# Attention, Fourier mixing and two FFNs on one core: token transform over two tiles at once, exp's bias of two batches on GpSimd, second W1 by column halves, a new priority table

## The chip, the cores and the metric

The kernel runs on one core of a Trainium2 chip. The metric is the device time of one execution, in microseconds; the time of a kernel is the median of several runs. Engines are named as the profile names them: PE (TensorE), DVE (VectorE), ACT (ScalarE), POOL (GpSimd) and SP (SyncE, which issues all DMAs here).

## What is computed

Three stages follow each other, for 4 batches of 576 tokens:

```
scores = (q @ k.T) / 8                    # 8 heads of 64
keep the 32 largest of each row, the rest to -1e9
x = softmax(scores) @ v                   # heads side by side: [576, 512]
u = x + real(fft(fft(x, axis=1), axis=2))
x = u + relu(norm(u) @ w_ch1) @ w_ch2     # 512 -> 2048 -> 512
x = x + relu((norm(x) * g) @ w_ch1b) @ w_ch2b
```

The weights come in as 64-bit floats and are split on the chip into a high and a low half-precision part; products use three of the four combinations.

## The kernel before

**Tiles.** A batch's tokens lie in two pairs of 128-row tiles, `xA` and `xB` (each 128 x 2 x 512), and a rest of 64 rows in `xC`, which two batches share. Row pairs that the transform adds and subtracts lie in the same partition of `xA` and `xB`.

**Attention.** `attend` works on 128 rows of one head (a *round* here; 36 rounds a batch, 144 in all). PE makes the scores (`ps`), ACT copies them (`s`), DVE finds the 32 largest by four MAX8 (`mx`) and three MATCH_REPLACE8 (`w`). A one-column DVE instruction makes `nb`, the bias of exp (lines 850 and 851). ACT does Prelu (needs the 32nd largest only), then Exp (needs `nb`), then the half-precision copy `p`; POOL subtracts for the low part, SP transposes by DMA into `pt`, PE multiplies with `vt` into `xp`, ACT scales into the tiles. There are four buffers of `s`, and two each of `w`, `p` and `pt`. Before a batch's first round its scales (`sc`) must be known: `stats` loads q, k, v in 27 pieces, PE sums squares, `find_scales` ends on DVE. `prep` then scales and transposes q and k.

**Token transform.** `fourier_rows(b, half)` folds the rows (line 944): for the cosine and the sine part, and for each of the two 128-row tiles and the rest, one instruction adds or subtracts `xA` and `xB` (`z`), one folds `z` on itself (`f`), ACT copies one column, ACT writes the high part, DVE the low part (`unT`). Then PE multiplies with a constant matrix. `fourier_columns` finishes, `do_norm` prepares the first FFN.

**FFN.** `ffn` goes over 16 blocks of 128 hidden units, `f` = 0 to 15: 12 matmuls of the first weight, relu on ACT (`h`, and `hr` for the low part), then 6 matmuls of the second weight into `acc`, for tile pairs A and B and, every second batch, C.

**Weights.** Four weights, 1a, 2a (first FFN), 1b, 2b (second FFN). Each is fetched in 16 pieces, turned to 32-bit on ACT, DVE and POOL, its scale is found, and eight chunks are converted. For 1b ACT makes a scaled copy in `ws` (two buffers), then its high part, and POOL the low part. 1b is converted into the place (`W1B`) that serves 2b as staging before, so its pieces come after 2b.

**The order.** Nothing runs in the order in which the code is written. Every call is recorded, and `Program.order` (line 336) places all instructions with a planner: at each step the engine and the instruction that can start first by the planner's own costs (`price`, line 289), ties by a priority from `LEVELS` (ten numbers for each of 51 stages: five levels, five slopes) and earliest times from `PACE` and `P.at`. The result is a fixed list for each engine, which the engine works through in order. In the trace all these instructions therefore have one line, 433.

Of the kernel before, what the change touches and what calls it, by code (L numbers as in the profile page):

```python
# [63 lines left out]
SMALL = "dve"  # L64
FLIP = "gp"
# [131 lines left out]
class Program:  # L197
# [91 lines left out]
    def price(self, op, out, reads, size, es):  # L289
# [11 lines left out]
        elif e == "vector":  # L301
            fast = op.method in ("tensor_scalar", "tensor_copy") and not psum
            fields = sum(isinstance(op.kw.get(k), View) for k in ("scalar", "scalar1", "scalar2"))
            op.cost = (168 if op.method == "match_replace" else 76 if op.method in ("tensor_scalar", "tensor_tensor") else 66) + 57 * fields + n / (1.92 if fast else 0.96)
        elif e == "scalar":
            fields = sum(isinstance(op.kw.get(k), View) for k in ("scale", "bias", "accum_out"))
            op.cost = (68 if psum else 110) + 0.834 * n + 94 * fields
        elif e == "gpsimd":
            half = any(v.at(0).dtype in (F16, BF16) for v in reads + [out])
            if op.method in ("tensor_tensor", "scalar_tensor_tensor"):  # L310
                op.cost = 650 if n < 4 else 168 + 1.886 * n if half else 160 + 2.12 * n
            elif op.method in ("tensor_scalar", "tensor_copy"):
# [23 lines left out]
    def order(self):  # L336
# [29 lines left out]
        while todo:  # L366
# [27 lines left out]
            if op.eng == "tensor":  # L394
                k = int(t // window)
                if columns.get(k - 1, 0) < enough:
                    op.cost *= 2
                k = int((t + op.cost) // window)
                columns[k] = columns.get(k, 0) + op.columns
# [36 lines left out]
class _Engine:  # L436
    def __init__(self, prog, name):
        self._p, self._n = prog, name

    def __getattr__(self, method):  # L440
        return lambda *a, **k: self._p.record(self._n, method, a, k)


@with_exitstack
def tile_attention_fourier_ffn(ctx: ExitStack, tc: tile.TileContext, q, k, v, w1a, w2a, g, w1b, w2b, c1_in, c2_in, c2l_in, out):
    nc = tc.nc
    outf = out.rearrange("b s d -> (b s) d")
    P = Program(tc, ctx)
    pe, dve, act, gp, sp = P.pe, P.dve, P.act, P.gp, P.sp
    sm, rv = getattr(P, SMALL), getattr(P, FLIP)  # L450
# [787 lines left out]
```

## Time and profile before

| | us |
|---|---|
| median of 3 runs (1319.77 to 1326.45) | 1324.66 |
| the profiled execution | 1330.46 |
| its span, first to last instruction | 1328.7 |
| busy: PE / DVE / ACT / POOL | 1182.6 / 993.0 / 846.0 / 680.2 |
| mean granted clock of PE | 0.940 |

The profile has one execution. Its rows give busy time by stretch (windows), by instruction shape (groups), in order of time (timeline), and the chain of work that ended last. PEclk is the granted clock as a share of 2.4 GHz. A busy PE is not PE at its peak: matmuls overlap, so a row's mean duration is longer than the step from one matmul to the next.

### The profile page before, as it was taken

The page shows a single profiled execution, that of the slowest core. Times are in us where ns is not written, and L with a number is a line of the kernel's source. Part 1 is how long each engine was busy: PE and PEld are TensorE (multiplying, and loading weights), DVE is VectorE, ACT ScalarE, POOL GpSimd, SP SyncE. Part 2 cuts the span into 40 slices and gives each one's busy share as a digit, 9 for nine tenths or more (in the row PEclk, how much of TensorE's full clock was granted, in tenths as well). Part 3 has the DMA queues.
Part 4 walks back from the last instruction along what each step waited for, and adds up shares of the span by engine and source line. Part 5 has one row for each costly group of instructions (what it writes and reads, how often), then busy time and mean ns, then how long its engine had stood idle before and what let it go on. Part 6 is the DMA issues. An engine that isn't in the chain of part 4 may idle for free.

```text
span 1328.7 us, 27154 instructions
## 1 busy us (share of the span) xinstructions
PE 1182.6 (89%) x9422; PEld 748.8 (56%) x9422; DVE 993.0 (75%) x2361; ACT 846.0 (64%) x1888; POOL 680.2 (51%) x1015
## 2 busy tenths in 40 slices
PE   7757888676799749999999999979999999999998
PEld 3433444342566525656666766656666666667665
DVE  6999999939899998999967986999996651214112
ACT  4658888467878897787767786777777652122111
POOL 3666343646777776666756564766645452011000
PEclk9999788578799869999999999999999999999999
DMA  6898655978867656876826376699514735014112
GB/s 186 193 263 222 178 129 122 264 189 234 196 162 158 121 120 153 174 170 141 177 62 110 68 175 164 141 217 189 105 22 97 163 90 129 13 24 126 27 33 56
DMA packets 356085, 184.86 MB, mean 139 GB/s; under 512 B 293225, under 2 KB 321002, under 8 KB 355818
## 3 DMA queue, kind: packets, MB, share of 16 engines
q1 hardware_dynamic: 355946, 183.11, 59.0%
q8 instruction: 74, 1.21, 0.4%
q14 instruction: 65, 0.53, 0.1%
HBM read 101.78 MB, written 14.16 MB: 87 GB/s over the span
## 4 chain that ended last, share of the span: by engine, by line
PE 63%; DVE 11%; DMA 7%; ACT 6%; issue 2%; POOL 2%; SPq 2%; POOLq 0%; ACTq 0%; DVEq 0%
PE mm L433 31%; PE acc L433 24%; PE ps L433 4%; PE xp L433 4%; DVE mx L433 4%; DVE w L433 3%; DMA pt<-p 2%; DMA ws<-W2D 2%; ACT s L433 2%; SPq L433 2%; DMA W1B<-in_moe_w_ch_dram 2%; DVE tiny L433 1%; DVE W1B L433 1%; DVE W2A L433 1%; ACT W1B L433 1%
## 5 line engine op out<-in xcount | busy, mean ns | idle before, releaser
L433 DVE MAX8 mx<-w 128x8 f32<-128x576 f32 x432 | 314.3, 747 | 1.3
L433 POOL TENSOR_TENSOR p<-s,p 128x64 f16<-128x64 f32 (+1 forms) x288 | 208.1, 743 | 118.2 <-ACT p L433 106.5
L433 ACT ACTIVATE h<-mm 128x256 f16<-128x256 f32 (+1 forms) x320 | 115.7, 362 | 212.7 <-PE mm L433 181.0
L433 PEld LDWEIGHTS <-h 128*128 128x128 f16 x1728 | 161.7, 98 | 141.6 <-issue 7.0
L433 PE MATMUL mm<-unT,W1B 128*128 128x256 f16 (+1 forms) x1920 | 220.7, 263 | 6.0 <-ACT W1B L433 3.4
L433 PE MATMUL mm<-unT,W1A 128*128 128x256 f16 (+1 forms) x1920 | 221.3, 263 | 1.1 <-DMA unT<-t2k 0.6
L433 PE MATMUL acc<-W2A,h 128*128 128x512 f16 x864 | 216.9, 379 | 1.4 <-POOL h L433 1.2
L433 POOL TENSOR_TENSOR h<-hr,h 128x256 f16<-128x256 f32 (+1 forms) x224 | 143.9, 646 | 140.1 <-ACT h L433 78.9
L433 PEld LDWEIGHTS <-W1B 128*128 128x128 f16 (+1 forms) x1984 | 176.8, 99 | 67.3 <-POOL W1B L433 13.9
L433 DVE MATCH_REPLACE8 w<-mx,w 128x576 f32<-128x576 f32 x288 | 212.8, 740 | 0.0
L433 PEld LDWEIGHTS <-W1A 128*128 128x128 f16 (+1 forms) x1984 | 177.5, 99 | 60.1 <-POOL W1A L433 8.1
L433 PE MATMUL acc<-ws,h 128*128 128x512 f16 x654 | 165.9, 380 | 6.2 <-DMA ws<-W2D 5.6
L433 DVE SCALAR_TENSOR_TENSOR h<-mm,h 128x256 f16<-128x256 f32 (+1 forms) x96 | 36.4, 379 | 171.8 <-ACT h L433 142.9
L433 DVE MAX8 mx<-s 128x8 f32<-128x576 f32 x144 | 107.5, 747 | 53.9 <-ACT s L433 53.6
L433 ACT ACTIVATE s<-s,mx 128x576 f32<-128x576 f32 x144 | 111.0, 773 | 22.2 <-DVE mx L433 21.9
L433 ACT ACTIVATE hr<-mm 128x256 f32<-128x256 f32 (+1 forms) x224 | 82.1, 368 | 65.0 <-PE mm L433 53.8
L433 PE MATMUL xp<-vt,pt 128*128 128x65 f16 (+1 forms) x2240 | 106.0, 203 | 16.5 <-DMA pt<-p 13.7
L433 PEld LDWEIGHTS <-pt 128*128 128x128 f16 (+1 forms) x2240 | 94.6, 107 | 44.9 <-DMA pt<-p 22.9
L433 ACT ACTIVATE s<-ps 128x576 f32<-128x576 f32 x144 | 93.6, 650 | 39.9 <-POOL p L433 21.8
L433 DVE MATCH_REPLACE8 w<-mx,s 128x576 f32<-128x576 f32 x144 | 106.6, 740 | 0.0
L433 PE MATMUL ps<-kt,qt 128*128 128x512 f16 (+5 forms) x512 | 90.2, 320 | 18.3 <-ACT s L433 18.2
L433 ACT ACTIVATE p<-s 128x576 f16<-128x576 f32 x144 | 97.6, 683 | 2.4 <-DMA pt<-p 1.9
(155 smaller groups left out, 1643.2 us busy)
## 6 DMA issues: line engine op xcount, KB each, us to landing
ws<-W2D SPq DMA_DIRECT2D x118, 256.0 KB
W1B<-in_moe_w_ch_dram SPq DMA_DIRECT2D x56, 512.0 KB
n<-in_q_dram SPq DMA_DIRECT2D x32, 128.0 KB
n<-in_k_dram SPq DMA_DIRECT2D x32, 128.0 KB
n<-in_v_dram SPq DMA_DIRECT2D x32, 128.0 KB
W2F<-W1B SPq DMA_DIRECT2D x16, 256.0 KB
ws<-in_moe_w_ch_dram SPq DMA_DIRECT2D x16, 256.0 KB
W1B<-W2F SPq DMA_DIRECT2D x16, 256.0 KB
```

The lines of the kernel that those rows point to most:

```text
L433: getattr(getattr(self.nc, op.eng), op.method)(*[fix(a) for a in op.args], **{k: fix(v) for k, v in op.kw.items()})
```

## The change

Five things change.

1. `fourier_rows` does both 128-row tiles with one instruction each: `z`, `f`, the column copy, the high and the low part. The 64-row rest keeps its own.
2. `nb` of batches 0 and 1 is made on POOL instead of DVE: 72 instructions of one column move.
3. 1b's eight chunks are converted in the order 0, 2, 4, 6, 1, 3, 5, 7: first those that hold the first half of the hidden units.
4. The planner's costs: a MATCH_REPLACE8 is 56 ns cheaper, and a matmul that it takes to be at the low clock costs twice its time plus 25 ns. The constants' earliest time goes from 183 to 210.
5. `LEVELS` and `PACE` have other numbers throughout.

```
-SMALL = "dve"
+SMALL = (0, 1)
...
-PACE = {'1a': (7.0, 4.0, 60.0, 6.5), '2a': (8.0, 5.0, 88.0, 1.5), '2b': (31.0, 10.0, 0.0, 8.5), '1b': (87.0, 14.0, 119.0, 9.5), 's1': (83.0, 4.5, 230, 0.5), 's2': (127.0, 3.0, 670, 8.0), 's3': (3.0, 1.0, 100, 2.5)}
+PACE = {'1a': (0.0, 3.5, 23.0, 1.0), '2a': (3.0, 6.5, 150.0, 8.5), '2b': (4.0, 3.5, 0.0, 2.0), '1b': (30.0, 13.0, 253.0, 0.0), 's1': (54.0, 7.0, 230, 0.5), 's2': (227.0, 5.0, 670, 8.0), 's3': (47.0, 0.0, 100, 2.5)}
...
-            op.cost = (168 if op.method == "match_replace" else 76 if op.method in ("tensor_scalar", "tensor_tensor") else 66) + 57 * fields + n / (1.92 if fast else 0.96)
+            op.cost = (112 if op.method == "match_replace" else 76 if op.method in ("tensor_scalar", "tensor_tensor") else 66) + 57 * fields + n / (1.92 if fast else 0.96)
...
-                    op.cost *= 2
+                    op.cost = 2 * op.cost + 25
...
-        for c in range(8):
-            P.at(t1 + c * step1, (nm, 2, c))
+        for i, c in enumerate(range(8) if nm != "1b" else (0, 2, 4, 6, 1, 3, 5, 7)):
+            P.at(t1 + i * step1, (nm, 2, i))
...
-            parts = [tmps(2 * c + j) for j in range(2)]
+            parts = [tmps(2 * i + j) for j in range(2)]
...
-        sm.tensor_scalar(out=nb, in0=mx[:, 31:32], scalar1=mx[:, 0:1], scalar2=scale(b, "c"), op0=ALU.subtract, op1=ALU.mult)
+        (gp if b in SMALL else dve).tensor_scalar(out=nb, in0=mx[:, 31:32], scalar1=mx[:, 0:1], scalar2=scale(b, "c"), op0=ALU.subtract, op1=ALU.mult)
...
+            z = P.tile("t2k", [128, 2, 257], F32)
+            f = P.tile("t2k", [128, 2, 129], F32)
+            if half:
+                eng.tensor_tensor(out=z, in0=x["A"][:, :, 128:385], in1=x["B"][:, :, 128:385], op=op, claim=xf)
+                eng.tensor_tensor(out=f[:, :, 0:128], in0=z[:, :, 0:128], in1=z[:, 0, 256:257].dims((257, 2), (-1, 128)), op=op)
+                act.activation(out=f[:, :, 128], in_=z[:, :, 128], func=AF.Copy)
...
+            act.activation(out=xf[:, cs, 0:2, 0, 0:n], in_=f[:, :, 0:n], func=AF.Copy, scale=sv)
+            dve.scalar_tensor_tensor(out=xf[:, cs, 0:2, 1, 0:n], in0=f[:, :, 0:n], scalar=sv, in1=xf[:, cs, 0:2, 0, 0:n], op0=ALU.mult, op1=ALU.subtract)
...
-        P.at(183)
+        P.at(210)
```

Three places show what the new numbers do to the order.

DVE, from batch 0 to batch 1. Names: `sc_272` are batch 1's scales, `s_174` and `s_175` score buffers, `unT`, `Y`, `xA`, `xB` belong to batch 0's transform, `BN_STATS` to its norm. Before, the last rows ahead of batch 1's first MAX; its scales stand 22 rows ahead of that MAX:

```order
L433 TENSOR_TENSOR Y_211<-mm_253,Y_211 128x320
L433 SCALAR_TENSOR_TENSOR t2k_221<-mm_253,sc_271,t2k_222 128x257 x2
L433 TENSOR_TENSOR xA_196<-xA_196,t2k_221 128x257
L433 TENSOR_TENSOR xB_201<-xB_201,t2k_221 128x257
L433 SCALAR_TENSOR_TENSOR t2k_223<-mm_253,sc_271,t2k_220 128x257 x2
L433 TENSOR_TENSOR xA_196<-xA_196,t2k_223 128x257
L433 TENSOR_TENSOR xB_201<-xB_201,t2k_223 128x257
L433 BN_STATS tiny_116<-xA_196 128x6
L433 SCALAR_TENSOR_TENSOR t2k_220<-mm_253,sc_271,t2k_222 64x257 x2
L433 MAX mx_128<-s_174 128x8
```

In the change, from the last row of those scales:

```order
L433 TENSOR_SCALAR sc_272<-sc_272 128x1
L433 MAX mx_131<-w_182 128x8
L433 TENSOR_SCALAR tiny_116<-xp_247,sc_271 64x2
L433 TENSOR_SCALAR tiny_122<-xp_247,sc_271 128x4
L433 RECIPROCAL tiny_116<-tiny_116 64x2
L433 RECIPROCAL tiny_122<-tiny_122 128x4
L433 MAX mx_128<-s_174 128x8
L433 MATCH_REPLACE w_181<-mx_128,s_174 128x576
L433 MAX mx_129<-s_175 128x8
L433 MAX mx_128<-w_181 128x8
L433 MATCH_REPLACE w_182<-mx_129,s_175 128x576
L433 MATCH_REPLACE w_181<-mx_128,w_181 128x576
```

Batch 1's first rounds now stand ahead of batch 0's second half of the transform, where they stood behind it and behind the first BN_STATS.

POOL, near the end of batch 0's rounds. Names: `p_186<-s_174` is the low part of `p`, `W1B_91<-W1B_91` the last step of 2b's turning to 32-bit, `tiny_...<-mx_...` is `nb`. Before:

```order
L433 TENSOR_TENSOR W1B_91<-W1B_91 128x512 x4
L433 TENSOR_TENSOR p_187<-s_177,p_187 128x512
L433 TENSOR_TENSOR p_187<-s_177,p_187 128x64
L433 TENSOR_TENSOR W1B_91<-W1B_91 128x512
L433 TENSOR_TENSOR p_186<-s_174,p_186 128x512
L433 TENSOR_TENSOR p_186<-s_174,p_186 128x64
L433 TENSOR_TENSOR W1B_91<-W1B_91 128x512 x2
L433 TENSOR_TENSOR p_187<-s_176,p_187 128x512
L433 TENSOR_TENSOR p_187<-s_176,p_187 128x64
```

In the change:

```order
L433 TENSOR_TENSOR W1B_91<-W1B_91 128x512 x4
L433 MEMSET vt_169 128x5
L433 TENSOR_TENSOR vt_169<-n_136,vt_169 128x5x64
L433 TENSOR_SCALAR tiny_122<-mx_131 128x1
L433 TENSOR_SCALAR tiny_117<-mx_128 128x1
L433 TENSOR_SCALAR tiny_115<-mx_129 128x1
L433 TENSOR_TENSOR W1B_91<-W1B_91 128x512
L433 TENSOR_TENSOR p_187<-s_177,p_187 128x512
L433 TENSOR_TENSOR p_187<-s_177,p_187 128x64
L433 TENSOR_TENSOR W1B_91<-W1B_91 128x512 x2
L433 TENSOR_TENSOR p_186<-s_174,p_186 128x512
L433 TENSOR_TENSOR p_186<-s_174,p_186 128x64
```

The one-column `nb` stands in the same queue as the subtractions and the weight's additions, and the queue is worked through in order.

ACT, where the second W1 is converted, from the first scaled copy on. Names: `ws_...<-W1B_91,tiny` is the scaled copy, `W1B_91<-ws` the high part, `hr` and `h` are relus of the first FFN. Before:

```order
L433 ACTIVATE ws_239<-W1B_91,tiny_118 128x512
L433 ACTIVATE vt_169<-n_135 128x5x64
L433 ACTIVATE W1B_91<-ws_239 128x512
L433 ACTIVATE hr_215<-mm_252 128x256
L433 ACTIVATE h_233<-mm_252 128x256
L433 ACTIVATE s_175<-s_175,tiny_121,sc_272 128x576
L433 ACTIVATE s_177<-s_177,tiny_119,sc_272 128x576
L433 ACTIVATE p_186<-s_175 128x576
L433 ACTIVATE hr_216<-mm_253 128x256
L433 ACTIVATE h_234<-mm_253 128x256
L433 ACTIVATE p_187<-s_177 128x576
L433 ACTIVATE qt_156<-qb_152 128x256
```

In the change:

```order
L433 ACTIVATE ws_238<-W1B_91,tiny_124 128x512
L433 ACTIVATE ws_239<-W1B_91,tiny_124 128x512
L433 ACTIVATE W1B_91<-ws_238 128x512
L433 ACTIVATE W1B_91<-ws_239 128x512
L433 ACTIVATE hr_216<-mm_252 128x256
L433 ACTIVATE h_233<-mm_253 128x256
L433 ACTIVATE s_176<-s_176,mx_130 128x576
L433 ACTIVATE ws_238<-W1B_91,tiny_124 128x512
L433 ACTIVATE h_234<-mm_252 128x256
L433 ACTIVATE W1B_91<-ws_238 128x512
L433 ACTIVATE ws_239<-W1B_91,tiny_124 128x512
L433 ACTIVATE hr_215<-mm_251 128x256
```

Before, the conversion is spread between rounds of attention; in the change the copies come in pairs, close together, with relus of the first FFN between them. From the first scaled copy to the first relu of the second FFN stand 104 ACT instructions before, and 59 in the change.

## Rows read from the trace of the kernel before

**Rows 1.** The page's first line.
```profile
span 1328.7 us, 27154 instructions
```

**Rows 2.** Windows by stage, all engines: stretch, its length, then busy us per engine.
```profile
0.00:272.70 272.70, 204.25 (x1137) 105.26 (x1137) 245.22 (x562) 184.94 (x348) 137.95 (x171) 0.86 0.72 193
272.70:304.60 31.90, 28.32 (x167) 14.04 (x167) 12.05 (x36) 21.52 (x53) 16.52 (x29) 0.86 0.73 197
304.60:443.00 138.40, 117.39 (x974) 75.31 (x972) 132.16 (x329) 113.37 (x252) 98.41 (x145) 0.90 0.77 184
443.00:499.30 56.30, 29.92 (x269) 17.42 (x268) 55.52 (x128) 52.81 (x106) 43.16 (x60) 0.70 0.62 121
499.30:1051.00 551.70, 530.30 (x4785) 352.54 (x4783) 475.03 (x1118) 408.28 (x956) 343.01 (x559) 0.99 0.64 136
1051.00:1328.70 277.70, 272.46 (x2104) 184.27 (x2101) 73.02 (x194) 65.12 (x176) 41.19 (x53) 1.00 0.27 67
```

**Rows 3.** DVE timeline 255 to 305 us: start, us, instruction, idle time before.
```profile
258.54 0.20 DVE L433 TENSOR_SCALAR tiny<-mx 128x1 f32<-128x1 f32 x1
258.66 0.17 DVE L433 RECIPROCAL tiny<-tiny 128x4 f32<-128x4 f32 x1
...
277.43 0.16 DVE L433 TENSOR_SCALAR tiny<-mm 128x3 f32<-128x3 f32 x1 [4.41 <-PE mm L433]
...
278.30 0.28 DVE L433 COPY sc<-tiny 128x2 f32<-128x2 f32 x3
...
304.57 0.74 DVE L433 MAX8 mx<-s 128x8 f32<-128x576 f32 x1
```

**Rows 4.** The chain that ended last: start, us, what.
```profile
470.38 1.32 DVE mx L433 x2
471.70 1.46 DVE w L433 x2
...
1153.67 2.59 PE acc L433 x12
1156.26 2.62 PE mm L433 x24
```

**Rows 5.** Timeline around the second W1's scale and the second FFN's first relu.
```profile
442.91 0.14 DVE L433 COPY wsc<-tiny 128x4 f32<-128x4 f32 x1
...
499.33 0.36 ACT L433 ACTIVATE h<-mm 128x256 f16<-128x256 f32 x1
```

**Rows 6.** Groups by shape, GpSimd and ScalarE around the bias: busy us, mean ns, idle before.
```profile
L433 POOL TENSOR_TENSOR p<-s,p 128x512 f16<-128x512 f32 x144 | 167.6, 1164 | 87.0 <-ACT p L433 82.1 <-issue 1.4 <-POOL h L433 1.1
...
L433 ACT ACTIVATE s<-s,mx 128x576 f32<-128x576 f32 x144 | 111.0, 773 | 22.2 <-DVE mx L433 21.9
...
L433 POOL TENSOR_SCALAR n<-n,sc 128x320 f32<-128x320 f32 x80 | 44.8, 562 | 54.2 <-DMA n<-in_v_dram 22.9 <-DMA n<-in_k_dram 14.0 <-DMA n<-in_q_dram 4.0
...
L433 POOL TENSOR_TENSOR W1B<-W1B 128x512 int32<-128x512 int32 x24 | 32.3, 1357 | 22.2 <-DVE W1B L433 15.5 <-PE xp L433 2.7 <-ACT p L433 2.6
...
L433 POOL TENSOR_TENSOR tiny<-tiny,mhalf 128x2 f32<-128x2 f32 x16 | 11.6, 729 | 74.5 <-DVE tiny L433 74.1
...
L433 DVE TENSOR_SCALAR tiny<-mx 128x1 f32<-128x1 f32 x36 | 7.0, 197 | 0.1
```

**Rows 7.** Groups by shape, ScalarE in the conversion of the second W1.
```profile
L433 ACT ACTIVATE ws<-W1B,tiny 128x512 f32<-128x512 f32 x16 | 11.4, 717 | 0.7 <-DVE tiny L433 0.7
...
L433 ACT ACTIVATE W1B<-ws 128x512 f16<-128x512 f32 x16 | 9.9, 624 | 0.1
```

**Rows 8.** Groups by shape, operations that the token transform merges.
```profile
L433 DVE SCALAR_TENSOR_TENSOR t2k<-mm,sc,t2k 128x257 f32<-128x257 f32 x16 | 7.0, 480 | 5.4 <-ACT t2k L433 2.9 <-PE mm L433 2.5
...
L433 DVE SCALAR_TENSOR_TENSOR unT<-t2k,sc,unT 128x129 f16<-128x129 f32 x16 | 6.8, 424 | 8.0 <-ACT unT L433 6.1 <-POOL n L433 1.7
```

**Rows 9.** Windows with a low granted clock: columns as in group 2, then clock and DMA.
```profile
232.40:265.60 33.20, 22.41 (x124) 11.77 (x124) 31.78 (x70) 15.62 (x28) 21.49 (x22) 0.50 0.92 266
431.00:499.30 68.30, 41.92 (x376) 25.82 (x373) 67.11 (x157) 61.97 (x125) 51.62 (x72) 0.75 0.60 120
```

More of the change, by code (lines that the diff above doesn't have):

```diff
@@ L449, in tile_attention_fourier_ffn @@
     pe, dve, act, gp, sp = P.pe, P.dve, P.act, P.gp, P.sp
-    sm, rv = getattr(P, SMALL), getattr(P, FLIP)
+    rv = getattr(P, FLIP)
     const = ctx.enter_context(tc.tile_pool(name="const", bufs=1))
@@ L952, in fourier_rows @@
         for cs, (eng, op) in enumerate(((gp if b in FSUM else dve, ALU.add), (gp, ALU.subtract))):
-            for t in range(3):
-                pr = slice(0, 128) if t < 2 else ck
-                if t < 2:
-                    u, w = x["A"][:, t, :], x["B"][:, t, :]
-                    z = P.tile("t2k", [128, 512], F32)
-                    if half:
-                        zc, cols = z[:, 128:385], lambda a: a[:, 128:385]
-                    else:
-                        cols = lambda a: a.rearrange("p (a c) -> p a c", a=4)[:, 0:4:3, :]
-                        zc = cols(z)
-                    eng.tensor_tensor(out=zc, in0=cols(u), in1=cols(w), op=op, claim=xf)
-                else:
-                    z = x["C"][pr]
-                f = P.tile("t2k", [128, 129], F32)[pr]
-                if half:
-                    eng.tensor_tensor(out=f[:, 0:128], in0=z[:, 128:256], in1=z.rev(384, 128), op=op)
-                    act.activation(out=f[:, 128:129], in_=z[:, 256:257], func=AF.Copy)
-                else:
-                    eng.tensor_tensor(out=f[:, 1:128], in0=z[:, 1:128], in1=z.rev(511, 127), op=op)
-                    act.activation(out=f[:, 0:1], in_=z[:, 0:1], func=AF.Copy)
-                act.activation(out=xf[pr, cs, t, 0, 0:n], in_=f[:, 0:n], func=AF.Copy, scale=sv[pr])
-                dve.scalar_tensor_tensor(out=xf[pr, cs, t, 1, 0:n], in0=f[:, 0:n], scalar=sv[pr], in1=xf[pr, cs, t, 0, 0:n], op0=ALU.mult, op1=ALU.subtract)
@@ new lines, in fourier_rows @@
+            z = P.tile("t2k", [128, 2, 257], F32)
[4 more added lines that the diff above has]
+                act.activation(out=f[:, :, 128], in_=z[:, :, 128], func=AF.Copy)
+            else:
+                ends = lambda a: a.rearrange("p t (a c) -> p t a c", a=4)[:, :, 0:4:3, :]
+                zz = z[:, :, 0:256].rearrange("p t (a c) -> p t a c", a=2)
+                eng.tensor_tensor(out=zz, in0=ends(x["A"]), in1=ends(x["B"]), op=op, claim=xf)
+                eng.tensor_tensor(out=f[:, :, 1:128], in0=z[:, :, 1:128], in1=z[:, 0, 255:256].dims((257, 2), (-1, 127)), op=op)
+                act.activation(out=f[:, :, 0], in_=z[:, :, 0], func=AF.Copy)
@@ new lines, in fourier_rows @@
+            act.activation(out=xf[:, cs, 0:2, 0, 0:n], in_=f[:, :, 0:n], func=AF.Copy, scale=sv)
+            dve.scalar_tensor_tensor(out=xf[:, cs, 0:2, 1, 0:n], in0=f[:, :, 0:n], scalar=sv, in1=xf[:, cs, 0:2, 0, 0:n], op0=ALU.mult, op1=ALU.subtract)
+            z = x["C"][ck]
+            f = P.tile("t2k", [128, 129], F32)[ck]
+            if half:
+                eng.tensor_tensor(out=f[:, 0:128], in0=z[:, 128:256], in1=z.rev(384, 128), op=op)
+                act.activation(out=f[:, 128:129], in_=z[:, 256:257], func=AF.Copy)
+            else:
+                eng.tensor_tensor(out=f[:, 1:128], in0=z[:, 1:128], in1=z.rev(511, 127), op=op)
+                act.activation(out=f[:, 0:1], in_=z[:, 0:1], func=AF.Copy)
@@ L975, in fourier_rows @@
+            act.activation(out=xf[ck, cs, 2, 0, 0:n], in_=f[:, 0:n], func=AF.Copy, scale=sv[ck])
+            dve.scalar_tensor_tensor(out=xf[ck, cs, 2, 1, 0:n], in0=f[:, 0:n], scalar=sv[ck], in1=xf[ck, cs, 2, 0, 0:n], op0=ALU.mult, op1=ALU.subtract)
         if not half:
```

2 lines of the change are left out of this document (1 added, 1 removed).

## The prediction

> **What bounds the kernel now.** I read the windows by stage first [rows 2], because the page's shares hide that the limit changes. Up to 272.7 us DVE is busy 245.22 us of 272.70: batch 0's rounds and the turning of the weights fill it. From 272.7 to 304.6 it is busy 12.05 of 31.90: the one large hole. From 304.6 to 499.3 it is full again, 132.16 of 138.40 and 55.52 of 56.30. From 499.3 on the picture turns over: PE is busy 530.30 of 551.70 and then 272.46 of 277.70, nearly always at the full clock, and DVE has 76.7 us to spare up to 1051. So DVE, with a wait in it, decides when PE can be filled, and PE decides the rest. The reader should see two facts in this. A DVE instruction saved after 499.3 is worth nothing by itself. And what is gained must show in the moment at which PE fills, which is the first relu of the second FFN, at 499.33 us [rows 5].
>
> Next, the order. At that relu both kernels stand alike: PE has 220 score matmuls of 560 and 36 FFN blocks around it, DVE has done some 65 rounds of 144. The work left on PE is the same. So the sum is made at this mark, and the rest is carried over.
>
> **The change, part by part.**
>
> *The second W1's scale.* The conversion can't start before DVE has written it, at 442.91 us [rows 5]. In the order 225 MAX8 and 169 MATCH_REPLACE8 stand ahead of it before, and 252 and 188 in the change: it comes some 6.75 rounds later in DVE's list. In the chain a MAX8 takes 0.66 us (1.32 for two) and a MATCH_REPLACE8 with its load 0.73 (1.46 for two) [rows 4]: 27 x 0.66 + 19 x 0.73 = 31.7 us more. All 54 bias instructions ahead of it leave DVE. A row's mean is 197 ns [rows 6], but the next small instruction starts 0.12 us later [rows 3]; bounds 54 x 0.12 = 6.5 and 54 x 0.2 = 10.8, I take 8. Some of batch 1's first transform half now stands ahead too: four low parts of two tiles each (below) and their neighbours, about 3 us. Together +27.
>
> *The hole between batch 0 and batch 1.* Before, batch 1's scales are written at 278.30, and its first MAX8 runs at 304.57 [rows 3]; between them DVE waits for the steps of batch 0's transform. In the change the order puts that MAX8 six rows behind the scales, ahead of the transform, so only batch 1's own preparation lies between. ACT has 24 instructions to do there, score copy included; in the old hole it did 53 in 21.52 us [rows 2], so about 10 us, and 12 with PE and the transposes. DVE has under 2 us of own work meanwhile. The idle time in the hole goes from 31.90 - 12.05 = 19.9 to about 10: -10 us. Bounds: -14 if the 4.41 us wait for PE's scale matmuls [rows 3] goes as well, -3 if the preparation is held up by the weights' DMAs. The later transform steps are then hidden behind rounds.
>
> So the scale comes at 442.9 + 27 - 10 = 460, with 63 rounds done instead of 56.
>
> *The conversion.* From that scale to the relu 56.4 us pass before, and ACT is busy 52.81 of them [rows 2, 5]: it is the limit there, with 104 instructions. In the change 59 stand between. 16 scaled copies of 717 ns and 15 high parts of 624 ns [rows 7] are 20.8 us; the 28 others, mostly relus of the first FFN and a few steps of attention, at the old stretch's mean of 52.81 / 106 = 0.5 us, are 14. I take 34 us, bounds 31 (rows overlap a little) and 42 (POOL's low parts, with two buffers, pace the pairs). 460 + 34 = 494, so **-5 us at the mark**.
>
> *The order of 1b's chunks.* The first blocks of the second FFN need chunks 0, 2, 4, 6, which now come first. But the list holds ACT to nearly the end of the conversion before the first relu, so I count nothing for it; what it could give is a rival.
>
> *Both tiles in one instruction.* For each half, batch and part, one DVE instruction replaces two of 424 ns; the nearest row of double length is 480 ns for 257 columns [rows 8]. That is 0.37 us for each of 16, 6 us on DVE, and about as much on ACT and POOL together. Three of the four batches lie behind the mark, where PE is the limit; only the chain from the last round to PE's transform matmuls becomes shorter, some 0.5 us in each of six halves: -3 us, bounds 0 and -6.
>
> *The bias on POOL.* The trace has no such instruction on POOL. The nearest rows are 562 ns for 320 columns with the same kind of scalar, and 729 ns for two columns of a power [rows 6]; from below 197 ns, what DVE needs. I take 0.4 us, nearest to the first: 72 x 0.4 = 29 us on an engine that is idle 190 of the first 443 us [rows 2]. ACT's Prelu of 773 ns covers it if it is not queued. Nothing counted, up to +20 as a rival.
> The Trainium skill, GPSIMD Engine Reference, section 4.1 (Engine selection), says that elementwise work belongs on VectorE and that GpSimd is the slower choice. By it the bias should have stayed on DVE, and the sum at the mark would be 8 us worse on DVE but without the queue's risk. The trace agrees on the single instruction; which side weighs more no row here shows.
>
> *Later.* PE idles 21.4 us from 499.3 to 1051 [rows 2]. The new list shuffles all of it; bounds -10 and +10, none counted.
>
> **Sum:** -5 - 3 = -8 us against the profiled execution's 1330.46 us, of which 1328.7 are its span [rows 1], so 1322.5. That execution is 0.4% above the median of the runs, 1324.66; against the median **1317 us**.
>
> **The rivals.**
>
> *A. Nothing to measure.* The gain at the mark is spent again: DVE's hole stays near 20 us, or PE's gaps after it grow by what was won. For it: the mark's gain is a difference of large terms, +27 + 12 - 40. Against it: the first MAX8 visibly moves ahead. 1322 to 1328.
>
> *B. Slower: the bias is late.* It stands behind a weight's addition of 1357 ns or a subtraction of 1164 ns in POOL's list [rows 6]. Then Exp waits 1.36 + 0.4 - 0.77 = 1 us, and ACT, working in order, with it. Some 60 rounds up to the mark make 60 us of ACT idle, of which the early stages can take two thirds (ACT is idle 123 us up to 443 [rows 2]). It decides once score buffers are freed too late for the next MAX8: 20 us at the mark, 1342.
>
> *C. Slower: the first FFN at half clock.* Its 32 blocks run at 2.6 us each at the full clock (2.59 and 2.62 for two halves of two [rows 4]); in the change they are spread over more rounds. Where PE was thinly loaded the granted clock was 0.50, its low level of 1.2 GHz, with PE busy 22.41 of 33.20 us, and 0.75 from 431 to 499.3 [rows 9]. At 1.2 GHz the blocks take 83 us more; PE's slack ahead of the mark is at most the 34 us of the conversion, so beyond 40% of the blocks it costs time: at three quarters, 62 - 34 = 28 us, 1345.
> The Trainium skill, TensorE: Matmul & The Clock Gate, Part 1, says that the throttled clock is the default and that activity releases it. The trace agrees with both levels [rows 9].
>
> *D. Faster: the split works.* If the second FFN's blocks start once half of the chunks are there, the mark is 17 us earlier, half of the 34: 1300.
>
> **How the numbers follow.** About 0.5% (6.6 us) can be told from no change. My forecast gets 0.5; its own bounds, 1305 to 1327, hold about two thirds below 1318. A 0.17, B 0.11, C 0.08, D 0.14. Faster: 0.33 + 0.14 + a little of A = 0.48. Same: 0.17 + 0.15 = 0.32. Slower: B, C = 0.2. The range reaches from 1299 (D) to 1336, which leaves out most of B and C.
>
> **What would show it.** Right: DVE's idle time around the batch change about 10 us, the second W1's scale near 460 us, 34 us to the first relu after it, PE as full as before from about 494. Wrong: Exp waiting for POOL's bias by more than 20 us in total (B); PEclk below 0.8 in the first FFN (C); the relu before 485 (D); the mark early but PE idle over 30 us behind it (A).

## The result, and the profile after

The changed kernel is slower: 1333.87 us (median of 5 runs, 1333.33 to 1340.13) against 1324.47 us for the kernel before in the same comparison; ratio 1.0071, interval 1.0044 to 1.0098. The profiled execution took 1333.87 us itself. The kernel before ran once more with a profile; that execution took 1324.66 us, the median, where the one read ahead of the prediction took 1330.46. All times of "before" below come from this second profile, unless a row group is named. A profile is one execution: the two of the unchanged kernel before lie 2.0 us apart at the third weight scale (271.5 and 269.4) and 4.0 us at the fourth (442.9 and 438.9), so a difference of this size between two single profiles shows nothing by itself.

Windows by stage of the second profile of the kernel before (as in [rows 2]: stretch, length, busy us of PE, PEld, DVE, ACT, POOL, then granted clock, DMA share, GB/s). The bounds are its third weight scale, batch 1's first MAX8, its fourth weight scale and the first relu of the second FFN (the mark):

```profile
0.00:269.40 269.40, 203.21 (x1132) 103.66 (x1132) 243.65 (x558) 183.47 (x346) 136.78 (x171) 0.86 0.73 194
269.40:301.20 31.80, 27.48 (x170) 13.75 (x171) 13.20 (x40) 22.45 (x54) 16.52 (x29) 0.92 0.79 205
301.20:438.90 137.70, 117.72 (x974) 75.66 (x973) 132.75 (x327) 112.92 (x252) 98.75 (x145) 0.90 0.77 184
438.90:495.30 56.40, 29.27 (x268) 16.84 (x266) 55.62 (x129) 52.92 (x108) 43.07 (x60) 0.73 0.60 123
495.30:1051.00 555.70, 533.16 (x4848) 354.58 (x4845) 476.52 (x1120) 411.84 (x963) 347.02 (x564) 1.00 0.65 137
1051.00:1322.90 271.90, 266.69 (x2042) 180.09 (x2040) 71.94 (x191) 61.59 (x169) 38.00 (x48) 1.00 0.26 64
```

The same windows of the changed kernel, at the same events:

```profile
0.00:276.10 276.10, 208.97 (x1148) 106.06 (x1148) 241.92 (x527) 184.12 (x342) 143.30 (x202) 0.85 0.69 192
276.10:290.00 13.90, 11.02 (x80) 6.06 (x81) 2.10 (x14) 11.32 (x25) 5.69 (x10) 0.81 0.74 157
290.00:470.70 180.70, 135.86 (x1081) 81.24 (x1080) 174.44 (x389) 145.46 (x321) 132.76 (x216) 0.86 0.75 175
470.70:501.90 31.20, 28.85 (x211) 17.77 (x210) 19.51 (x47) 30.85 (x62) 26.21 (x29) 1.00 0.25 52
501.90:1051.00 549.10, 526.65 (x4779) 351.61 (x4779) 462.96 (x1089) 401.31 (x932) 345.28 (x558) 1.00 0.67 141
1051.00:1332.10 281.10, 272.93 (x2129) 185.06 (x2126) 79.75 (x202) 67.15 (x178) 42.27 (x53) 1.00 0.28 67
```

Length less DVE's busy time is its idle time, and the ledger follows:

| stretch | before | changed | difference | forecast |
|---|---|---|---|---|
| up to the third scale | 269.4 | 276.1 | +6.7 (work -1.7, idle +8.4) | none |
| third to fourth scale, DVE's work | 145.9 | 176.5 | +30.6 | +27 |
| third to fourth scale, DVE's idle time | 23.6 | 18.1 | -5.5 | -10 |
| fourth scale to the mark | 56.4 | 31.2 | -25.2 | -22.4 |
| behind the mark | 827.6 | 830.2 | +2.6 | -3 |
| sum | 1322.9 | 1332.1 | +9.2 | -8.4 |

The forecast of +27 was for all of DVE's work up to the fourth scale; measured there it is 30.6 - 1.7 = +28.9.

DVE's timeline of the changed kernel has the two holes of which the ledger speaks, and the scales (start, us, instruction, idle time before it and what ended it):

```profile
208.11 0.76 DVE L433 MAX8 mx<-s 128x8 f32<-128x576 f32 x1 [11.32 <-ACT s L433]
...
276.12 0.15 DVE L433 COPY wsc<-tiny 128x4 f32<-128x4 f32 x1
...
287.42 0.34 DVE L433 TENSOR_SCALAR tiny<-xp,sc 64x2 f32<-64x2 f32 x2 [9.97 <-PE xp L433]
...
289.80 0.76 DVE L433 MAX8 mx<-s 128x8 f32<-128x576 f32 x1 [1.82 <-ACT s L433]
...
470.71 0.15 DVE L433 COPY wsc<-tiny 128x4 f32<-128x4 f32 x1
```

The second hole is the one forecast (9.97 + 1.82 us, in place of 18.6 between the third scale and the first MAX8 before). The first, 11.32 us in batch 0, stands in no step of the prediction. The mark follows the last scaled copy of the conversion; ACT's timeline of the changed kernel:

```profile
501.06 0.72 ACT L433 ACTIVATE ws<-W1B,tiny 128x512 f32<-128x512 f32 x1
501.88 0.38 ACT L433 ACTIVATE h<-mm 128x256 f16<-128x256 f32 x1
```

And the bias on POOL, groups by shape of the changed kernel (busy us, mean ns, idle before), which answer to [rows 6]:

```profile
L433 POOL TENSOR_SCALAR tiny<-mx,sc 128x1 f32<-128x1 f32 x36 | 13.7, 383 | 8.8 <-DVE mx L433 6.5 <-PE mm L433 1.7 <-DVE tiny L433 0.5
...
L433 POOL TENSOR_SCALAR tiny<-mx 128x1 f32<-128x1 f32 x36 | 10.6, 301 | 29.9 <-DVE mx L433 26.2 <-DVE tiny L433 3.6
```

### The profile page after: what moved, and what is told of

Its sections match the earlier page's. It is cut to its first block, busy times and chain, and to the rows that moved or that the text cites. A ratio compares the mean times of both kernels' runs of the same rounds, so it can differ in the third digit from the quotient of the medians.

```text
span 1332.1 us, 27081 instructions
## 1 busy us (share of the span) xinstructions
PE 1184.3 (89%) x9422; PEld 747.8 (56%) x9422; DVE 980.7 (74%) x2261; ACT 840.2 (63%) x1856; POOL 695.5 (52%) x1067
## 5 line engine op out<-in xcount | busy, mean ns | idle before, releaser
L433 PE MATMUL acc<-W2A,h 128*128 128x512 f16 x864 | 213.9, 380 | 3.4 <-POOL h L433 3.2
L433 PE MATMUL acc<-ws,h 128*128 128x512 f16 x654 | 164.9, 379 | 11.9 <-DMA ws<-W2D 11.4
L433 PE MATMUL ps<-kt,qt 128*128 128x64 f16 (+5 forms) x512 | 88.2, 311 | 19.5 <-ACT s L433 19.1
L433 ACT ACTIVATE s<-s,tiny,sc 128x576 f32<-128x576 f32 x108 | 93.5, 873 | 6.5 <-DVE tiny L433 4.5
```

The costliest lines, as they stand in the source:

```text
L433: getattr(getattr(self.nc, op.eng), op.method)(*[fix(a) for a in op.args], **{k: fix(v) for k, v in op.kw.items()})
```

## The experiments

Two kinds of edit are used. "Order kept" means that the planner's list is made first and then patched, so that every instruction not named stands where it stood. "Order anew" means that the planner runs again.

**The kernel before again.** 

> The kernel before, unchanged, for a second profile: the one read ahead of the prediction took 1330.46 us, 6 us over the median of its runs. If those 6 us lie ahead of the first relu of the second FFN (499.3 us there), it comes at 493 to 496 us here, and the change then lost 6 to 9 us ahead of that place; if they lie behind it, it comes at 498 to 501 us and the change lost its time behind that place. Time 1320 to 1327 us.

1324.66 us. The mark comes at 495.3 us. Of the 5.8 us between the spans of the two profiles 4.0 lie ahead of it and 1.8 behind. Of the changed kernel's 9.2 us, 6.6 are lost ahead of the mark.

**One part alone, order kept.** First the bias.

```diff
         self.placed = self.order()
+        for _, op in self.placed:
+            if op.eng == "gpsimd" and op.method == "tensor_scalar" and out is "tiny" and in0 is "mx":
+                op.eng = "vector"
```

> The changed kernel with the bias of all four batches on VectorE; the order of everything else on every engine is kept. Theory (the bias on GpSimd is cheap and the time lies in the new order): VectorE gets 36 x 0.197 + 36 x 0.260 = 16.5 us of work back, of which batch 0's share partly fills idle time and batch 1's 9.4 us lies ahead of the fourth weight scale on a full VectorE: first relu of the second FFN 4 to 12 us later than 501.9 us, time 1334 to 1342 us. Rival (the wait of the exp for GpSimd's queue is what made the hole of 11.3 us in batch 0 and the lost time): the hole is under 5 us and the time is 1320 to 1328 us.

1347.79 us, ratio 1.0154 [1.012, 1.0187], so 0.8% slower than the changed kernel, and by more than the theory said. Third scale at 284.9, mark at 514.1, +12 us. The hole stays (10.97 us at 212.6). The rival falls: POOL's queue does not make the hole.

In the kernel before, where `nbs` are the 144 bias instructions:

```diff
         self.placed = self.order()
+        for op in nbs[:72]:
+            op.eng = "gpsimd"
```

> The kernel before with the bias of batches 0 and 1 on GpSimd, at the same places of the same order. Theory (cheap on GpSimd): VectorE loses 16.5 us of work, some 7 to 9 us of it ahead of the fourth weight scale: 1314 to 1325 us. Rival (the exps wait for GpSimd's queue): round ends of batch 0 and 1 fall behind by 5 us or more, 1328 to 1340 us.

1335.32 us, ratio 1.0066 [1.0043, 1.009]: slower, as the rival had it. The profile is the slowest of its runs, 1344.59 us, 9 us over the median, so its rows show a larger loss than the median has. ACT's waits up to the fourth scale in this kernel, and in the changed one (engine, what waits, for what: us, times, longest):

```profile
ACT s L437 <- POOL tiny L437: 11.1, 10, 5.2
```
```profile
ACT s L433 <- POOL tiny L433: 6.8, 4, 2.8
```

In an order made for a bias on DVE, the exps wait 11.1 us for POOL in 36 + 18 rounds; in the order made for POOL, 6.8 us in 62 or so. That these waits make the loss is not shown. Batch 1 alone (`nbs[36:72]` in place of `nbs[:72]`):

> The kernel before with the bias of batch 1 alone on GpSimd, order kept. Both batches together cost 9 us there, with +8.2 us already at the 24th round. Theory (the loss is made in batch 0, where GpSimd also adds the weights' low words; in batch 1 the move saves VectorE 18 x 0.12 to 0.26 us ahead of the fourth scale): 1320 to 1328 us, fourth scale within 3 us of 438.9. Rival (GpSimd's queue holds up the exps in any batch): fourth scale 443 to 450 us, 1329 to 1336 us.

1331.18 us, ratio 1.0051 [1.0032, 1.007]. The time is the rival's, but the fourth scale (441.7) is the theory's. The mark comes at 500.1 us, 4.8 us after that of the kernel before, but only 0.8 after that of its first profile (499.3): where the time is lost stays open. And batch 0's bias alone back on VectorE in the changed kernel (`"vector"` for the first 36 only):

> The changed kernel with the bias of batch 0 alone back on VectorE, order kept. Both batches together cost 14 us there, +8.8 us at the third scale and +3.1 more at the fourth. Theory (in the new order each bias on VectorE stands in front of a full engine and holds up the exps): third scale at 281 to 287 us, time 1339 to 1346 us. Rival (as in the order of before, batch 0's bias on GpSimd is the costly one): third scale at 268 to 274 us, time 1322 to 1331 us.

1344.39 us, 1.0151 [1.0123, 1.0179], third scale at 285.5: as expected. So the same move, the bias of both batches to POOL, is a gain of 0.8% in one order and a loss of 0.7% in the other.

Then the transform, in the changed kernel split again into two instructions each:

```diff
-    call(**{k: fix(v) for k, v in op.kw.items()})
+    for j in range(2):                      # op is one of the 80 merged ones
+        call(**{k: part(v, j) for k, v in op.kw.items()})
```

> The changed kernel with each instruction on both 128-row tiles split into two again, order kept. Theory (the merged forms are worth little): VectorE gets about 6 us and ScalarE about 8 us back over the whole span, about a quarter of it ahead of the first relu of the second FFN: 0 to +4 us, 1332 to 1339 us. Rival (a merged instruction holds up its readers, which begin on one tile only): 1326 to 1331 us.

1338.76 us, 1.0089 [1.0054, 1.0123]; the interval holds the changed kernel's ratio, so no cost is shown. In the profiles the mark is 3.7 us later, and 2.5 us more are lost behind it. Merged alone in the kernel before, at the place of the second instruction of each pair (the changed kernel's transform, all else as before, and the list of the kernel before with each pair's first instruction dropped):

```diff
-    -> z(t=0) -> f(t=0) -> z(t=1) -> f(t=1)
+    -> z(both) -> f(both)                   # at the places of z(t=1), f(t=1)
```

> The kernel before with the merged transform alone: each pair of instructions on the two 128-row tiles becomes one at the place of the second; the order of all others and the buffers are kept. Theory (worth what undoing it cost in the new order, 4.9 us, of it 3.7 ahead of the first relu of the second FFN): that relu at 491 to 494 us (495.3), time 1318 to 1324 us. Rival (at the place of the second, the first tile's readers wait): 1325 to 1331 us.

1338.09 us, 1.01 [1.0076, 1.0123]. Slower, as the rival had it, and by more than it said. In the profile (1342.97 us, 4.9 over the median) most of it lies behind the mark: 840.1 us instead of 827.6, with PE waiting 5.6 us for ACT's high parts there, a wait of which the kernel before shows no row:

```profile
PE mm L631 <- ACT unT L631: 5.6, 7, 1.9
```

At the place of the first (those of `z(t=0)`, `f(t=0)`):

> The kernel before with the merged transform alone, each merged instruction at the place of the first of its pair (the run with the place of the second ended 18 us late in its profile: 5.8 us at the first relu of the second FFN, of which 4.8 stood there ahead of any changed instruction, and 12.5 us behind it). Theory (behind that relu the merged instruction at the second's place held up its readers on TensorE): the loss behind the relu falls to 0 to 3 us, time 1318 to 1330 us. Rival (the merged form itself costs in an order not made for it): loss behind the relu 8 us or more, time 1333 to 1342 us.

1332.55 us, 1.0058 [1.0036, 1.008]. Behind the mark 831.3 us, so 3.7 in place of 12.5 lost, and the wait is down to 2.3 us. But this profile took 1329.72 us, 2.8 under its median, and the other 4.9 over: by the medians the place is worth 5.5 us, less than half of what the merged form cost at the place of the second. A gain is not there either.

**The code and the numbers apart, order anew.** The changed code with the old priorities, pacing and costs (`LEVELS`, `PACE`, `P.at(183)`, 168 for a MATCH_REPLACE8, `op.cost *= 2`):

> The changed kernel's code (merged transform, bias on GpSimd, chunk order of 1b) with the numbers of before (priorities, pacing, start of the constants' loads, costs); the planner sets the order anew. Its order puts the fourth weight scale behind 54.75 rounds (56.25 in the kernel before, 63 in the changed one). Theory (the time follows the order, the code parts are worth 10 to 20 us on VectorE): fourth scale at 425 to 440 us, time 1312 to 1326 us. Rival (GpSimd's bias needs an order made for it, as the kernel before with that part alone showed by +9 us): 1330 to 1345 us.

1354.1 us, 1.0207 [1.0182, 1.0232]. The time is above both expectations. The scale comes at 440.8 and the mark at 493.0, near those of the kernel before (438.9 and 495.3), and 31 us are lost behind the mark. The old code with the new numbers, the same lines the other way round:

> The kernel before's code with the changed kernel's numbers; the planner sets the order anew, and puts the fourth weight scale behind 62.75 rounds. Theory (the new numbers put the scale late, and the old code adds the 14 us that the bias on VectorE cost in the new order and 5 us of the split transform): fourth scale at 475 to 490 us, first relu of the second FFN 505 to 520 us, time 1340 to 1356 us. Rival (the new numbers by themselves are no worse): 1320 to 1332 us.

1404.29 us, 1.0599 [1.0577, 1.0622]. The fourth scale (484.2) and the mark (517.3) are in the range, the time is 48 us above it; PE's idle time behind the mark is 66.7 us, where it was 27.8 before. And the changed kernel with one row of the priorities put back:

```diff
-'x2a': (-635, -1001, -1001, -805, -198, 148, 57, 151, 55, -191)
+'x2a': (-423, -381, -359, -381, -276, 19, -71, 333, -45, 227)
```

> The changed kernel with one row of the priorities, that of the second weight's conversion (2a), as it was before; the planner sets the order anew. Theory (that row makes the hole in batch 0): no gap over 4 us on VectorE between 190 and 225 us, 30th round at 219 to 226 us (230.0), time 1320 to 1332 us if the rest of the order holds. Rival (another cause of the hole): a gap of 8 us or more in batch 0 again. As the whole order is set anew, the time alone says little here; the gap is what is asked.

1407.96 us, 1.0637 [1.0607, 1.0667], with a gap of 11.25 us again. So putting that row back does not remove the hole, and a new plan moves the time by 74 to 80 us here, more than any part of the change did. These plans made anew can't price a part.

**The hole in batch 0, order kept but for the instructions named.** ACT's exps, copies of `p` and score copies ahead of the conversion of weight 2a. In ACT's list (a piece; others moved likewise):

```diff
+ACTIVATE s_176<-s_176,tiny_121 128x576
+ACTIVATE p_186<-s_176 128x576
 ACTIVATE W2A_87<-W2A_87,wsc_279 128x512 x2
 ...
-ACTIVATE s_176<-s_176,tiny_121 128x576
-ACTIVATE p_186<-s_176 128x576
```

> The changed kernel with ScalarE's exps, copies of p and score copies of batch 0 pulled ahead of the second weight's conversion wherever their inputs are there (and GpSimd's low parts of p with them); TensorE, VectorE and the DMA queue keep their order. Theory (VectorE's idle 11.3 us in batch 0 comes from ScalarE's list, and what VectorE loses ahead of the fourth weight scale is lost at the end): the gap before the MAX8 at 208 us falls to 2 to 5 us, the 30th round ends at 221 to 225 us (230.0), the fourth scale comes at 461 to 467 us (470.7), the first relu of the second FFN at 492 to 498 us (501.9), time 1324 to 1330 us. Rival (the weight's conversion, now later, or batch 1's scales wait instead): batch 1's scales stay at 274 to 278 us, time 1331 to 1337 us.

1344.32 us, 1.0143 [1.012, 1.0167]. The gap is 7.5 us and later; batch 1's scales come 8.4 us later. Both expectations missed: the time is above the rival's too. With TensorE's scores (`ps<-kt,unT`) pulled ahead of `mm<-W2A` in the same way:

> As the run that closed the hole on ScalarE, but TensorE's score matmuls of batch 0 are pulled ahead of the second weight's conversion too, wherever their inputs are there. Theory A (the conversion of 2a must be done for the weights behind it; rounds pulled ahead of it only push it back, as the run with ScalarE alone showed with +8.4 us at the third scale): the gap of 11.3 us shrinks below 5 us, but the third weight scale comes at 280 to 288 us (276.1) and the time is 1336 to 1346 us. Theory B (the hole was lost time, and TensorE's order kept it open): third scale at 266 to 272 us, fourth at 460 to 466 us, time 1322 to 1330 us.

1340.17 us, 1.0114 [1.0089, 1.014]: theory A. The two gaps left are 3.1 and 4.4 us, the third scale comes at 280.9, and a new wait appears, of the next weight's (2b) first instruction on DVE. The three together are 13.3 us, more than the hole had:

```profile
DVE W1B L484 <- PE mm L484: 5.8, 1, 5.8
```

Here DVE waits for 2b's matmuls, which stand behind the conversion. In the changed kernel 2b's first matmuls follow 2a's last conversion step at once, and the third scale follows them by 50.5 us (PE's and DVE's timelines):

```profile
225.63 0.73 PE L433 MATMUL mm<-W1B 128*128 128x128 bf16 x10
...
276.12 0.15 DVE L433 COPY wsc<-tiny 128x4 f32<-128x4 f32 x1
```

In the kernel before, the same two:

```profile
218.88 1.09 PE L433 MATMUL mm<-W1B 128*128 128x128 bf16 x16
...
269.43 0.16 DVE L433 COPY wsc<-tiny 128x4 f32<-128x4 f32 x1
```

From one to the other pass 50.6 us. In 13 of the 17 profiles of kernels with one of the two orders it is 49.3 to 50.9 us, in the other four 52.9 to 55.4. A chain through 2b's matmuls would give such a constant time. So would a full DVE with the same list, and the windows speak for that in the changed kernel. First the kernel before, then the changed one, from the second scale to 2b's matmuls and from there to the third scale:

```profile
171.78:218.88 47.10, 42.20 (x233) 18.93 (x232) 42.47 (x97) 38.57 (x76) 12.66 (x21) 0.89 0.45 108
218.88:269.43 50.55, 30.31 (x212) 17.18 (x209) 46.16 (x105) 25.85 (x49) 30.73 (x30) 0.58 0.85 225
```
```profile
181.38:225.63 44.25, 39.56 (x181) 16.51 (x182) 31.51 (x68) 33.78 (x61) 9.14 (x17) 0.87 0.32 72
225.63:276.12 50.49, 33.58 (x248) 19.98 (x244) 49.79 (x117) 27.10 (x50) 32.58 (x39) 0.65 0.90 259
```

In the changed kernel DVE is idle for 0.7 of the 50.5 us, so from 225.6 us on its own work takes the time; in the kernel before it is idle for 4.4 of 50.6. The four longer times are those of the two runs in the changed order that put batch 0's bias on DVE and of the two that pull rounds ahead. To test the chain, the low parts of 2a were left out, 48 matmuls and 16 copies on ACT (written here as an edit of the kernel's lines):

```diff
-pe.matmul(out=ps, lhsT=sid, rhs=x, start=True, stop=False)
 act.activation(out=hi, in_=x, func=AF.Copy, scale=s)
-pe.matmul(out=ps, lhsT=nident, rhs=hi, start=False, stop=True)
-act.activation(out=lo, in_=ps, func=AF.Copy)
+gp.memset(lo, 0.0)
```

In the changed kernel

> The changed kernel without the low parts of the second weight (2a): the 48 matmuls that work them out are left out, and GpSimd writes zeros in place of ScalarE's 16 copies; the order is kept. Theory (the hole in batch 0 is the time of 2a's conversion on TensorE and ScalarE, and the third scale hangs from the conversion's end, where the 2b matmuls of the next scale begin): conversion over in 25 us or less instead of 43, the gap at 208 us under 4 us, third scale 262 to 268 us (276.1), time 1316 to 1326 us. Rival (VectorE's own work sets the third scale, the gap moves elsewhere): third scale at 272 us or later, time 1328 to 1336 us.

and in the kernel before.

> The same taken out of the kernel before, order kept. If the conversion's place in the new order is what made batch 0 slower, this kernel gains at least 4 us less at its third scale (269.4) than the changed one does, 0 to 5 us, and its time is 1319 to 1326 us. If both gain alike, the 6.7 us come from the later second scale (171.8 against 181.4 us) alone.

1334.58 us, 1.0061 [1.0043, 1.008], and 1327.92 us, 1.0015 [0.9993, 1.0036]. In the changed kernel the conversion ends at 217.8 (225.4), 2b's matmuls begin at 220.2, the third scale comes 50.8 us later at 271.0. This fits a chain, but the hole ends 4.7 us sooner too (203.4), so it fits a full DVE as well. The theory's other numbers missed: the conversion took 37 us and not 25, the hole is 7.8 us and not under 4, the scale lies between the two ranges, and the time, which does not change, in the rival's. Of the 5.2 us gained 3.8 are spent again by the fourth scale, 2.5 of them in the hole between the batches, DVE's timeline of that kernel:

```profile
284.80 0.34 DVE L439 TENSOR_SCALAR tiny<-xp,sc 64x2 f32<-64x2 f32 x2 [12.51 <-PE xp L439]
```

It is 12.51 us now, not 9.97, and the fourth scale is 1.4 us sooner, not 5.2. In the kernel before the same edit brings 2.8 us at the third scale: the changed kernel gains 2.4 us more there, less than the 4 asked for. But that profile took 1322.26 us, 5.7 under its median, and against the first profile of the kernel before the gain is 4.8 us. So the two gains can't be told apart, and what the conversion's place has to do with the 6.7 us is not shown. Last, the second scale itself sooner, and the conversion with it (VectorE's `W2A<-W1B` and scale instructions ahead of MAX8s, then `mm<-W2A` and `W2A<-mm` ahead of scores and exps):

> The changed kernel with VectorE's instructions up to the second weight's scale (2a), and then that weight's conversion on ScalarE and TensorE, pulled ahead of batch 0's rounds as far as their inputs allow; the rest keeps its order. Theory (chain of the weights: second scale, conversion, 2b matmuls, third scale): second scale at 174 to 178 us (181.4), conversion over at 216 to 221 us (224.8), third scale 269 to 273 us, time 1326 to 1332 us. Rival (the rounds that now stand behind pay for it, as in every other edit of an order): third scale 277 us or later, time 1336 to 1346 us.

1342.93 us, 1.0128 [1.0099, 1.0157]: the rival. The scale came at 176.1, but the conversion still ended at 225.5 and the hole grew to 12.7 us; 2b's matmuls began at 232.3 and the third scale came 50.8 us behind them, at 283.1.

**TensorE's activity in batch 0, order kept.** Three matmuls without use ahead of the scores of rounds of batch 0. The expectation says 34 rounds; the traces have 54 added matmuls, so 18 rounds, the first at 132.4 us in the kernel before:

```diff
+for _ in range(3):
+    pe.matmul(out=ps[:, 0, :], lhsT=nident, rhs=nident.unsqueeze(1).to_broadcast([128, 4, 128]), start=True, stop=True)
 pe.matmul(out=ps[o0:o0 + m, 0, :], lhsT=w, rhs=kt[:, 0:512], start=True, stop=stop)
```

In the kernel before:

> The kernel before with three matmuls without use (128 x 128 weights of the identity, 512 columns, 16 bit) ahead of the scores of each of 34 heads' halves of batch 0, into the same PSUM buffer, which the scores then overwrite. Theory (in batch 0 TensorE's clock decides how fast the order runs: the 32-bit score matmul takes 1.06 us at the low level and 0.59 us at the high one, and the runs that lost time show more of them slow): the share of slow matmuls between 100 and 285 us falls by half or more, third weight scale at 262 to 267 us (269.4), time 1314 to 1321 us. Rival (TensorE's clock in batch 0 is a by-product; VectorE sets the pace): the added 34 x 3 x 0.2 to 0.4 us of TensorE work is lost in part: third scale 270 to 278 us, time 1326 to 1338 us.

1336.84 us, 1.008 [1.0051, 1.0109]. The 18th round ends 3.2 us sooner, but the 12th ended 2.7 us sooner already, ahead of the first added matmul, so this is not the filler's. From there to the third scale, at 274.1, 7.9 us are lost. In the changed kernel:

> The changed kernel with the same filler. Theory (clock): the gap of 11.3 us at 208 us shrinks to under 7 us, third scale at 266 to 272 us (276.1), time 1324 to 1330 us. Rival (by-product): third scale 277 to 285 us, time 1335 to 1346 us.

1339.99 us, 1.0101 [1.0073, 1.0128]; the hole is 11.31 us. Both times and both third scales are the rival's: this filler costs time. Theory (clock) was hardly put to the test, though: of the 38 `ps<-kt,unT` matmuls of 512 columns between 100 and 285 us, 13 still took over 0.8 us (most others 0.59 or 0.69) where 16 did in the kernel before, and 14 for 16 in the changed one. What a higher clock there would give stays open.

No kernel of the study beats the kernel before.

## Why the prediction was wrong

**What held.** DVE's work to the fourth scale came as forecast: the 27 MAX8 and 19 MATCH_REPLACE8 more, priced from [rows 4], less the bias, were to make +27 us, and it grew by 28.9. The conversion took 31.2 us where 34 were taken from [rows 7], since the list holds ACT to the end of the conversion, as the text said. The bias costs 0.30 to 0.38 us on POOL, taken as 0.4. In the changed order what happens ahead of the mark reaches the end nearly whole: over its eight edits with the order kept, the shift at the end is within 2.8 us of that at the mark (with the bias, the exps or the scores moved +12.2, +13.5 and +10.7 us at the mark and +12.5, +12.6 and +10.4 at the end). In the order of before it is not so: its six edits show 2.7 to 12.5 us more behind the mark. So the mark was a fair place for the sum in the changed order.

**The step that failed** is "So the scale comes at 442.9 + 27 - 10 = 460". It took everything up to 272.7 us as given, although the order of that stretch is new too. There the changed kernel has 1.7 us less DVE work, and 8.4 us more idle time (6.8 against the first profile of before). That idle time was put at nothing, for the reason that DVE fills this stretch. This was read from a share of the old order (245.22 of 272.70, [rows 2]), which the new order does not keep. Of the 8.4 us, 4.0 lie ahead of the second scale, 8.1 between it and 2b's first matmuls, where the hole of 11.32 us stands beside the conversion of 2a on PE and ACT, and 3.7 are won back behind them. From the hole's end on DVE is nearly full, so nothing takes up the loss. The second scale itself comes at 181.4 us, not 171.8: 23.5 rounds stand ahead of it where 22.75 stood, and DVE has 5.6 us more work there. This much the traces show. What makes the hole, and why neither moving rounds nor moving the scale wins the time back, is not settled: each edit made a new wait.

Forecast and ledger lie 17.6 us apart, and this term is the largest part, not all: 8.4 us here, 5.6 behind the mark, 4.5 in DVE's idle time between the third and fourth scale, 1.9 in its work; the conversion gave 2.8 back. Without the 8.4 the ledger would still show no gain (+0.8).

**The hole between the batches** is 11.8 us, as forecast within the two numbers given (10 and 12). But the 19.9 us it was set against were those of an execution 6 us over the median; with 18.6 before, 6.8 were won there, and 1.3 lost again behind it: -5.5 for -10.

**Behind the mark**, -3 for the merged transform stood alone. Splitting it again cost 2.5 us there, in one profile of each, where the two of the unchanged kernel before lie 1.8 us apart: the size is neither shown nor refuted. The whole stretch is 2.6 us longer. PE's work is the same (799.58 us for 799.85), and its idle time 30.6 for 27.8; waits for the second weight's DMAs grew most, 11.4 us for 7.3. "Bounds -10 and +10, none counted" holds it.

**The bias at nothing** was right for the changed kernel and wrong as a rule. Rival B (the bias late on POOL) did not come there: Exp waits 6.8 us for POOL, where its sign was more than 20. In the order of before, not made for it, the move costs 9 us, but that sign is not reached either (11.1 us). The row of the Trainium skill, GPSIMD Engine Reference, section 4.1, that puts elementwise work on VectorE, agrees with the single instruction (301 ns on POOL, 197 on DVE, [rows 6]) and with the run in the old order; the run with the bias back on VectorE in the new one, 0.8% slower, speaks against it. The row's factor of about 2 is for operations of two inputs, which the bias is not.

**The other rivals.** A (the gain at the mark spent again) did not come as told: there was no gain at the mark to spend, and PE's idle time behind it grew by 2.8 us. Its sum, +27 + 12 - 40, is not that of the prediction's terms either, 27 - 10 - 22.4. C (first FFN at half clock) did not come: the granted clock is 0.86 from 290.0 to 470.7 us, where the kernel before has 0.90, and 1.00 from there to the mark, where it has 0.73. The durations say the same: from 300 to 500 us the 384 matmuls of the first weight take 283 ns each, in the kernel before 276. D did not come either; the mark stands behind the 16th scaled copy.

**Fitted orders.** Of the twelve edits with the order kept that leave nothing out, none is faster than the kernel it starts from. All five of the kernel before are slower by 0.5 to 1%, also the two that only take work away. This was measured, not explained: what it shows is that the gain of a part in such a kernel is not its busy time.

## What to carry to other kernels

When a change brings a new order, draw the chain of each event that others hang from (here each weight scale) through all engines, and for all of the program, before any stretch is taken as given. That an engine is full in the old order is no proof that it will be full in the new one: look in the new lists for the places where it must wait for another engine's. Price a moved instruction only in an order that was made for it, and read every kernel, also those of the experiments, from a profile whose time is near its median.

## What was not expected of the hardware

**The same list runs at different speeds.** Up to 167 us the kernel before and the one with the merged transform have the same instructions, yet their 18th rounds end 4.8 us apart. One source is TensorE's clock. PE's timelines of the kernel before and of that kernel (four 32-bit score matmuls together, or two):

```profile
63.91 2.39 PE L433 MATMUL ps<-kt,unT 64*128 64x512 f32 x4 [1.21 <-ACT s L433]
...
107.44 1.29 PE L433 MATMUL ps<-kt,unT 64*128 64x512 f32 x4
```
```profile
108.05 2.39 PE L631 MATMUL ps<-kt,unT 64*128 64x512 f32 x4
...
112.83 1.15 PE L631 MATMUL ps<-kt,unT 64*128 64x512 f32 x2
```

In one the matmuls take the shorter time from 107 us on, in the other only from 113, after the same work. That makes 1.2 us by the 14th round. The rest comes in the next two rounds, where four 32-bit matmuls of the first weight's conversion take 1.98 us in the one and 3.78 in the other, and DVE then waits 2.8 us for PE:

```profile
124.77 1.98 PE L433 MATMUL mm<-W1A,xC 128*128 128x512 f32 x4
```
```profile
128.76 3.78 PE L631 MATMUL mm<-W1A,xC 128*128 128x512 f32 x4
```

The profile with the bias of both batches on POOL has 3.78 us there as well, and its 18th round ends 5.7 us late; so its early loss can't be put down to the bias alone.

**The record of the granted clock can miss a stretch.** Windows of the kernel before and of the one with batch 1's bias moved (columns as above):

```profile
20.00:100.00 80.00, 57.45 (x295) 31.31 (x294) 78.41 (x179) 50.66 (x96) 48.17 (x52) 1.00 0.83 224
```
```profile
20.00:100.00 80.00, 56.85 (x291) 31.00 (x290) 78.34 (x176) 49.50 (x95) 48.20 (x52) 0.50 0.82 221
```

The first says 1.00 and the second 0.50, while the four score matmuls take 2.39 us in both. Of 20 profiles only 3 record this stretch as low. The Trainium skill, TensorE: Matmul & The Clock Gate, section "Seeing it yourself", warns that these records are unreliable; the rows agree. The durations of matmuls of one shape tell the level.

**VectorE and GpSimd get in each other's way.** The same pair of instructions on DVE, `W2A<-W1B`, took 0.74 us in the kernel before and 1.40 with the bias on POOL, where POOL was at a low part of `p` (120.42 to 121.85 us):

```profile
118.89 0.74 DVE L433 TENSOR_SCALAR W2A<-W1B 128x512 int32<-128x512 int32 x2
```
```profile
121.07 1.40 DVE L437 TENSOR_SCALAR W2A<-W1B 128x512 int32<-128x512 int32 x2
```

The Trainium skill, SBUF — State Buffer, section "Who interferes with whom", says that such an instruction in its fast mode and one of GpSimd exclude each other for their whole length. The pair agrees. Over the kernel the 16 of them went from 415 to 520 ns each. In the changed kernel, with the same bias on POOL, they take 415 again, so the bias on POOL does not do it by itself.
